# Two sets of the length-64 transform at a time, amid `down`, with a group's steps begun in the batch in front

## The chip, the cores and the metric

The kernel runs on one core of a Trainium2 chip. The metric is the device time of one launch in microseconds (us), the median of the runs made. TensorE (PE in the profile) multiplies matrices, VectorE (DVE) adds and multiplies element by element, ScalarE (ACT) copies and applies functions, GpSimd (POOL) does some additions and issues stores, and SyncE (SP) issues most of the loads and stores.

## The reference

Two blocks in a row, all in float32, with 8 batches, 3008 rows and 256 channels:

```
X = rfft(x, axis=1);  y = irfft(X * (filt_r + 1j * filt_i), n=3008, axis=1)      # filter along the rows
h = max(y^T @ w_tok1, 0) @ w_tok2;   u = y + h^T                                 # mixer along the rows, 3008 -> 256 -> 3008
out = u + max(u @ w_ch1, 0) @ w_ch2                                             # mixer along the channels, 256 -> 1536 -> 256
```

## The kernel before

**The filter** writes 3008 as 47 x 64. A first stage multiplies by the length-64 transform (the stage that the change is about), a second stage does the rest forward, the product with the filter and the way back, and the last step back is made inside the mixer. The first stage leaves its result in DRAM (`z_tmp`), the second loads it and leaves its own (`g_tmp`), which the mixer loads as tiles `t4`.

**The mixer** works batch by batch. `mix` loops over the batches, over six column tiles m of a batch (`MT`; five of 512 rows, the last of 448) and over six pairs jp of channel blocks (`JP`): 36 *items* a batch, 288 in all. Each item issues, in this order:

- place 0: `up_first` (four matmuls into two pg banks) and `up_middle` for this item, then `h_sums` and part 0 of `down` for the item in front; in some items also `u_part`, which makes the next m's `u` (`u_quarter` in batches 1 to 7);
- place 1: `up_last` (three matmuls into the same pg banks, two VectorE additions that take them out, two ScalarE activations), and up to two steps of a list of small VectorE steps (`finish`, `v_steps`);
- place 1.5: part 1 of `down` has been issued, part 2 not yet;
- place 2: part 2 of `down`, in jp 0 the first two steps of `finish` for the m in front, and in some items again `u_part`.

In batches 1 to 7 `u_part` comes at (jp, place) = (2, 2), (3, 0), (3, 2) and (3, 2); for the next batch's first m at (4, 0) and (5, 0), two parts each. In the item with number 32 of a batch (m 5, jp 2), `token_product` for the next batch runs: twelve steps of seven matmuls, whose weights `w1` lie in a ring of seven buffers. Seven loads are issued by SyncE in the items ahead, and the other five within `token_product`, each when a buffer comes free.

**Filter beside mixer.** The batches form groups, `GROUPS = ((0,), (1, 2), (3, 4), (5, 6), (7,))`. While a group is mixed, the filter's steps of the next group run in between. `dft(bs)` is a generator: it yields a letter for the kind of step that comes next, and the main loop looks at each place of `mix` whether that kind is due there. The order is written out by hand: no planner and no costs.

For the last three groups (12, 12 and 6 units `todo`, a unit is four columns of one batch) the first stage is *tiled*: a *set* is four matmuls of 64x64 tiles, each 512 wide, that run side by side in the four quarters of TensorE (eight instructions in the profile, line 523, helper `four`). The functions that take part:

- `x_pair` loads a unit of x into one of three `filt` buffers, with six DMAs or a few more on SyncE (L481 to L486); `more(n)` does so for the next n units;
- `x_sums` makes the sum and the difference of the two halves on VectorE (L548, two operations) in `p1` or `p2`, by the unit's parity;
- `a_pair` takes the two banks acc and b (`turn`), issues the set, and calls `z_out` for each bank: a ScalarE copy (L539) into a tile `t1` (two buffers) and a DMA on SyncE to `z_tmp` (L541).

The banks acc and b are also those of `u_quarter` (L865, L843) and of `token_product` (L810), through `free_bank`, which takes them in turn; the two pg banks are those of `up_first` (L944) and `up_last` (L960); the second stage's `bi_pair` uses them too.

In the kernel before, step "a" of the first stage is due at place 1 of every item from the first item of a group on: the x loads of three units in the first item, the sums of the first unit in the second, and then in each item the sums of the next unit, one x load, and a set with its copies. "w" (loads of the second stage) may come at any place, and "b" (a unit of the second stage) in the tiled groups at place 1.5 of jp 1 and 4, in the last six items of a batch (`tail`) of jp 1 and 3. The second stage already issues two sets in a row there: `b_pair` into acc and b, and `bi_pair` of the unit in front into pg.

Of the kernel before, what the change touches and what calls it, by code (L numbers as in the profile page):

```python
# [55 lines left out]
GROUPS = ((0,), (1, 2), (3, 4), (5, 6), (7,))  # L56
# [71 lines left out]
def kernel(  # L128
# [11 lines left out]
    nc = tc.nc  # L140
# [41 lines left out]
    def bank(tag):  # L182
        return (psg if tag == "pg" else psum).tile([P, 512], FP32, tag=tag, name="ps_" + tag)
# [3 lines left out]
    turn = ["acc", "b"]  # L187
# [233 lines left out]
    begin, copy, middle, end = (iter(tiles) for _ in range(4))  # L421
# [98 lines left out]
    def four(outs, stat, mov):  # L520
        for i in range(2):
            for j in range(2):
                nc.tensor.matmul(outs(i, j), stat(i, j), mov(i, j), start=True, stop=True)  # L523

    def half_of(half, n=HALF):
        return slice(half * HALF, half * HALF + n)

    def a_unit(b, c):
        ps = bank(free_bank())
        nc.tensor.matmul(ps, wa0 if b == 0 else wa, xs.pop((b, c)).rearrange("p a d -> p (a d)"), start=True, stop=True)  # L530
        if b == 0:
            d0, c = divmod(c, NXC // 2)
            nc.scalar.copy(out=turned[:, ts(c, 2 * XC), ds(d0 * P, P)], in_=ps.rearrange("p (a d) -> p a d", d=P))
            return
        z_out(b, ps, c, nc.scalar)

    def z_out(b, ps, c, q):
        t1 = t1p.tile([P, XC, D], FP32, tag="t1", name="t1")
        nc.scalar.copy(out=t1.rearrange("p a d -> p (a d)"), in_=ps)  # L539
        g, i = place_of[b]  # L540
        q.dma_start(z_d[g][:, ts(c, XC), i, :], t1)  # L541

    def x_sums(b, c, i):
        t = xs.pop((b, c)).rearrange("p s a d -> p s (a d)")
        where = (p1p, p2p)[i % 2]
        sd = where.tile([P, 2, XC * D], FP32, tag="p%d" % (1 + i % 2), name="sd")
        for e, op in enumerate((ALU.add, ALU.subtract)):
            nc.vector.tensor_tensor(out=sd[:, e], in0=t[:, 0], in1=t[:, 1], op=op)  # L548
        return sd

    def a_pair(b, c, sd):
        pss = [bank(tag) for tag in turn]
        four(lambda h, e: pss[h][half_of(e)], lambda h, e: was[half_of(h), e], lambda h, e: sd[half_of(h), e])
        for h in range(2):
            z_out(b, pss[h], 2 * c + h, nc.sync)

    def dft(bs):
        first = bs[0] == 0
        nb = len(bs)
        tiled = bs not in GROUPS[0:2]  # L560
        todo = [(b, c) for b in bs for c in range(NXC // 2 if tiled else NXC)]
# [18 lines left out]
        def w_load(c):  # L580
            table_load(c)
            (filt_load if first else filt_pair)(c)
# [3 lines left out]
        def more(n, queue=None):  # L586
            for i, u in to_load[0:n]:
                (x_pair if tiled else x_load)(*u, i, queue)
            del to_load[0:n]
# [2 lines left out]
        if bs == GROUPS[1]:  # L592
            ahead.append(more)
        if not first:
            yield "a"
        if tiled:
            sd = x_sums(*todo[0], 0)
            yield "a"
        for i, u in enumerate(todo):
            if tiled:  # L600
                now, sd = sd, x_sums(*todo[i + 1], i + 1) if i + 1 < len(todo) else None
                more(1)
                a_pair(*u, now)
                yield "a" if i + 1 < len(todo) else "w"
                continue
            if first and i in (0, 2):
                w_load(i // 2)
            if first and i in (6, 8):
                table_load(i // 2 - 1)
            a_unit(*u)  # L610
            if bs != GROUPS[1] or i >= XB:
                more(1)
            yield "a" if i + 1 < len(todo) else "w"
            if first and (i + 1) % (NXC // 2) == 0:

                for d in range(i // (NXC // 2) * P, (i + 1) // (NXC // 2) * P, 16):
                    v = turned.rearrange("p s d -> p d s")[:, d:d + 16, :]
                    nc.vector.transpose(v, v)
# [49 lines left out]
        def b_pair(c):  # L668
            pss, wb, t2 = two_banks(turn), wbs[c], t2s[c]
            four(lambda h, i: pss[h][half_of(i)], lambda h, i: wb[half_of(h, KH), i], lambda h, i: t2[half_of(h, KH), i])  # L670
            return pss
# [32 lines left out]
        if not first:  # L704
            last = K2 // KC
            for c in range(last):
                pss = b_pair(c)
# [457 lines left out]
    with tc.manual_schedule():  # L1165
        nc.sync.dma_start(wa0, wa0_d)
        nc.vector.memset(turned[:, A:K2, :], 0.0)
        for t in filts:
            nc.vector.memset(t, 0.0)
        half = 0  # L1170
        second = dft(GROUPS[1])
        for i, _ in enumerate(dft(GROUPS[0])):
            if i == 0:
                nc.scalar.dma_start(wai_t, wait_d)
            k = i - NXC - 2

            if i < NXC:
                if i in (1, 3, 5, 7, 9):
                    start()
                if i == NXC - 1:  # L1180
                    copies()
                    for t, src in ((wa, wa_d), (was, was_d), (wai, wai_d), (ident, ident_d)):
                        nc.scalar.dma_start(t, src)
            elif k >= 0:
                if k == K2 - 5:
                    pause.append(True)
                while half < 2 * IN_B * (k + 1) // K2:
                    if half % 2:
                        convert_end()
                    else:  # L1190
                        convert_middle()
                    half += 1

                if 19 <= k < 25:
                    t4_load(0, k - 19, 0, PARTS[1])
                elif 26 <= k < 29:
                    for c in range(2):
                        t4_load(0, 2 * (k - 26) + c, PARTS[1], PARTS[2])
                elif k in (30, 31):
                    for c in range(3):  # L1200
                        t4_load(0, 3 * (k - 30) + c, PARTS[2], PARTS[3])
        pause.clear()

        fill(5)
        for c in range(A // TC4):
            t4_load(0, c, PARTS[3], P, (nc.sync, nc.gpsimd)[c % 2])
        both = wcp.tile([P, 2, JP, 7, P], FP32, tag="wc", name="wc")

        chan.extend((both[:, 0], both[:, 1]))
        next(second)  # L1210
        for i in range(IN_B, A // 2 + TC * W2G):
            convert()
            if i == A // 2 + BY_PE - 1:
                sum_up()
                acc = token_sums(0)

        ahead[0](XF, nc.gpsimd)
        h1s[0] = token_relu(0, acc)
        for dh in range(DH):
            convert()  # L1220
            u_part(0, 0, dh)
        for f in v_steps(0, 0):
            f()
        convert_end(False)
        for _ in range(XB):
            next(second)
        group, todo, done = -1, iter(()), True

        def next_ready(b):
            return done or b != GROUPS[group][-1]  # L1230

        coming = "a"
        n = MT * JP
        for b, i, place in mix(next_ready):
            if group + 1 < len(GROUPS) and b == GROUPS[group + 1][0]:
                if not done:
                    raise AssertionError("the filter's steps don't fit beside the mixer's")
                group += 1  # L1240
                done = group + 1 == len(GROUPS)
                todo = iter(()) if done else dft(GROUPS[group + 1]) if group else second
                coming = "a"
            if done:
                continue
            jp = i % JP
            if coming in "aw":
                due = place == 1 or (place != 1.5 if group == 0 else coming == "w")
            elif group:
                tail = i >= n - JP  # L1250
                due = (jp, place) in {"b": ((1, 1.5), (3 if tail else 4, 1.5)), "m": ((2, 2) if tail else (3, 1), (5, 1)),
                                      "i": ((0, 1.5), (3 if tail else 4, 1.5))}[coming]
            else:
                due = (jp - (coming == "i")) % JP in ((5, 1, 2, 3) if i < 4 * JP else (5, 0, 1, 2, 3)) and place == {"b": 1, "m": 2, "i": 0}[coming]
            if coming == "a" and group == 0 and i < JP - 1:
                due = {0: 2, 1: 0, 1.5: 0, 2: 1}[place]
            for _ in range(due):
                if not done:
                    coming = next(todo, "end")
                    done = coming == "end"  # L1260
# [30 lines left out]
```

## Time and profile before

| | |
|---|---|
| median of 3 runs | 2424.17 us (2424.15 to 2425.02) |
| the profiled execution | 2425.85 us, span 2424.1 us |
| granted TensorE clock | 0.995 |
| TensorE busy | 2382.0 us (98%), 12340 matmul instructions |
| VectorE busy | 1942.6 us (80%) |
| ScalarE, GpSimd busy | 686.5 us (28%), 619.6 us (26%) |
| line 523, sets of the first stage | 30, from 493.18 us on (batches 1, 3 and 5) |

A page of a profile gives busy times by engine, a chain of work that ended last, and groups of instructions by source line. A row of the timeline gives the start, the length, engine, line, operation, output tile and inputs, the shape and how many of the kind were merged; in brackets stands how long the engine was idle before it and what ended that. Matmuls are pipelined: the length of one overlaps the next, so distances between starts are what counts.

### The profile page before, as it was taken

Reading aid. Unit: us, or ns where it says so; the run is one execution under the profiler, and the core shown is the slowest. Engines: PE = TensorE matmul, PEld = TensorE weight load, DVE = VectorE, ACT = ScalarE, POOL = GpSimd, SP = SyncE. Lnnn points to the kernel's source line nnn. Section 1 sums busy time; section 2 is a strip of 40 time slices with the busy share of each in tenths; the row PEclk is TensorE's granted clock in tenths of the full one; section 3 lists DMA queues with packets and bytes.
Section 4 is the critical chain, followed back from the end, with each engine's and each line's share of the span. In section 5 each row is a group of like instructions: output and inputs, shape, how many; then the busy total and the mean of one; then the engine's idle time right before and its main releaser. Section 6 shows DMA issues by size and latency. Waiting matters only on the chain.

```text
span 2424.1 us, 35550 instructions
## 1 busy us (share of the span) xinstructions
PE 2382.0 (98%) x12340; PEld 1985.9 (82%) x12340; DVE 1942.6 (80%) x3684; ACT 686.5 (28%) x1355; POOL 619.6 (26%) x1115
## 2 busy tenths in 40 slices
PE   7999999999999999999999999999999999999998
PEld 4666676978888888987888888897889888898887
DVE  7798778787887888777888888877787788777776
ACT  5733322232222222123222222213221222222222
POOL 7476332113111211211121112112112112112121
PEclk8999999999999999999999999999999999999999
DMA  9975545544343322444344222434324221411100
GB/s 217 248 231 166 155 144 177 161 155 138 108 133 98 86 79 78 160 134 146 103 132 125 76 81 82 145 101 133 90 75 151 63 60 46 152 63 31 39 15 20
DMA packets 187420, 278.66 MB, mean 115 GB/s; under 512 B 35485, under 2 KB 125291, under 8 KB 187240
## 3 DMA queue, kind: packets, MB, share of 16 engines
q1 hardware_dynamic: 140952, 212.56, 29.1%
q0 software_dynamic: 34688, 53.83, 8.2%
q10 hardware_dynamic: 11600, 10.00, 1.3%
q8 instruction: 98, 1.61, 0.3%
q14 instruction: 82, 0.67, 0.1%
HBM read 193.52 MB, written 82.72 MB: 114 GB/s over the span
## 4 chain that ended last, share of the span: by engine, by line
PE 90%; DVE 4%; DMA 2%; ACT 1%; issue 1%; POOL 1%; SPq 0%; ACTq 0%; DVEq 0%; POOLq 0%
PE ps_po L978 33%; PE ps_pg L944 18%; PE ps_pg L960 14%; PE ps_b L523 4%; PE ps_b L810 3%; PE ps_acc L865 3%; PE ps_acc L810 2%; PE ps_b L865 2%; PE ps_b L843 2%; PE ps_acc L843 2%; PE ps_pg L523 1%; PE ps_b L759 1%; DVE t L922 1%; DVE hh L922 1%; DMA filt<-in_x_dram 1%
## 5 line engine op out<-in xcount | busy, mean ns | idle before, releaser
L1025 POOL DMA_DIRECT2D out_dram<-r x752 | 407.9, 550 | 1542.3 <-issue 1082.2
L922 DVE TENSOR_TENSOR hh<-ps_pg,s 128x512 f32<-128x512 f32 (+3 forms) x864 | 482.0, 585 | 184.3 <-ACT s L947 181.4
L965 ACT ACTIVATE hh<-hh 128x512 f32<-128x512 f32 (+1 forms) x576 | 347.7, 621 | 993.4 <-DVE hh L922 989.5
L978 PE MATMUL ps_po<-t,wc 128*128 128x256 f32 (+1 forms) x2304 | 553.5, 379 | 1.8 <-DVE t L922 1.8
L978 PEld LDWEIGHTS ps_po<-t,wc 128*128 128x128 f32 x2304 | 427.8, 190 | 122.6 <-issue 40.8
L978 PE MATMUL ps_po<-hh,wc 128*128 128x256 f32 (+1 forms) x1728 | 413.2, 375 | 1.0 <-POOL wc L382 0.8
L944 PE MATMUL ps_pg<-v,wc 128*128 128x256 f32 (+1 forms) x1728 | 413.3, 375 | 0.7 <-POOL wc L381 0.7
L944 PEld LDWEIGHTS ps_pg<-v,wc 128*128 128x128 f32 x1728 | 327.3, 190 | 41.3 <-DVE v L922 3.1
L978 PEld LDWEIGHTS ps_po<-hh,wc 128*128 128x128 f32 x1728 | 327.7, 190 | 39.6 <-POOL wc L382 2.0
L960 PE MATMUL ps_pg<-u,wc 128*128 128x256 f32 (+1 forms) x1152 | 292.9, 377 | 1.2 <-DVE hh L922 1.2
L922 DVE TENSOR_TENSOR t<-t,hh 128x256 f32<-128x256 f32 (+1 forms) x576 | 245.0, 425 | 19.8
L960 PEld LDWEIGHTS ps_pg<-u,wc 128*128 128x128 f32 x1152 | 216.7, 190 | 44.2 <-DVE hh L922 13.9
L922 DVE TENSOR_TENSOR s<-ps_pg,hh 128x512 f32<-128x512 f32 (+1 forms) x288 | 196.1, 681 | 30.0
L947 ACT COPY s<-ps_pg 128x256 f32<-128x256 f32 (+1 forms) x288 | 105.9, 368 | 362.7 <-PE ps_pg L944 360.5
L922 DVE TENSOR_TENSOR t<-hh 128x512 f32<-128x512 f32 (+1 forms) x288 | 195.0, 677 | 0.6 <-ACT hh L965 0.6
L944 PE MATMUL ps_pg<-u,wc 128*128 128x256 f32 (+1 forms) x576 | 169.3, 375 | 2.9 <-DVE hh L922 2.8
L960 PE MATMUL ps_pg<-v,wc 128*128 128x256 f32 (+1 forms) x576 | 168.8, 375 | 0.0
L944 PEld LDWEIGHTS ps_pg<-u,wc 128*128 128x128 f32 x576 | 108.1, 190 | 19.3 <-DVE hh L922 6.2
L922 DVE TENSOR_TENSOR u<-ps_acc,u 128x256 f32<-128x256 f32 (+1 forms) x84 | 46.2, 550 | 97.0 <-PE ps_acc L865 66.1
L960 PEld LDWEIGHTS ps_pg<-v,wc 128*128 128x128 f32 x576 | 109.1, 190 | 12.7
L922 DVE TENSOR_TENSOR u<-ps_b,u 128x512 f32<-128x512 f32 (+2 forms) x126 | 74.4, 591 | 28.9 <-PE ps_b L865 26.7
L865 PE MATMUL ps_acc<-w 128*128 128x256 f32 (+1 forms) x336 | 85.5, 377 | 1.0 <-ACT t L539 1.0
(152 smaller groups left out, 2661.9 us busy)
## 6 DMA issues: line engine op xcount, KB each, us to landing
w<-w_tmp SPq DMA_DIRECT2D x84, 448.0 KB
w<-w_tmp SPq DMA_DIRECT2D x35, 896.0 KB
out_dram<-r POOLq DMA_DIRECT2D x696, 32.0 KB, 2.5
t<-g_tmp SPq DMA_DIRECT2D x42, 512.0 KB
g_tmp<-t SPq DMA_DIRECT2D x96, 192.0 KB
t<-z_tmp SPq DMA_DIRECT2D x180, 96.0 KB
z_tmp<-t SPq DMA_DIRECT2D x60, 256.0 KB
filt<-in_x_dram SPq DMA_DIRECT2D x90, 128.0 KB
```

The costliest lines, as they stand in the source:

```text
L523: nc.tensor.matmul(outs(i, j), stat(i, j), mov(i, j), start=True, stop=True)
L759: nc.tensor.matmul(acc[:, t, :], w1[:, a, ts(t, P)], t4[b, a // TC4][:, a % TC4, :], start=(a == 0 and t == 0), stop=(a == A - 1 and t == ...
L810: nc.tensor.matmul(ps[:, at], w[:, n], mov, start=(j == 0 and i in (0, 2)), stop=(j == AP - 1 and i >= 5))
L843: nc.tensor.matmul(ps[:, ds(q * P, n)], t4[b, c][:, r, ts(dh, P)], wai[:, 0:n], start=(first and q == 0), stop=(not first and q == 3))
L865: nc.tensor.matmul(ps[:, ds(j * hw, hw)], h1[:, n, :], w2m[m % 2][:, at, 0:hw], start=(i < 2 and j == 0), stop=(j == len(todo) - 1))
L922: nc.vector.tensor_tensor(out=out, in0=in0, in1=in1, op=op)
L944: nc.tensor.matmul(ps[:, 0:hw], chan[0][:, jp, n, :], mov, start=True, stop=True)
L947: nc.scalar.copy(out=s[:, 0], in_=g[0][:, 0, 0:hw])
L960: nc.tensor.matmul(ps[:, 0:hw], chan[0][:, jp, n, :], mov, start=True, stop=True)
L965: nc.scalar.activation(out=hs, in_=hs, func=AF.Relu)
L978: nc.tensor.matmul(po[i][:, j, 0:hw], chan[1][:, jp, n, :], mov, start=(jp == 0 and first == 1), stop=(jp == JP - 1 and last == 1))
L1025: q.dma_start(bass.AP(tensor=ob.tensor, offset=ob.offset + row * D + g * cw, ap=[[N1 * D, 32], [D if h else -D, n], [1, cw]]), blocks[ts(g ...
```

## The change

The first stage's units are taken two at a time, and its one kind of step is split into three:

- "s": the sums of one unit (VectorE);
- "d": both sets, one behind the other, the first into acc and b (`turn`), the second into the two pg banks; then the copies and stores of the pg banks (`leave_pg`), and the x loads of two more units;
- "c": the copies and stores of acc and b (`leave`).

Outside of the tail "s" is due at (jp, place) = (0, 1), (2, 1), (3, 1), (5, 1), "d" at (1, 1.5) and (4, 1.5), "c" at (2, 0) and (5, 0). In the tail "s" is due at (3, 1), (4, 0), (5, 1), "d" at (4, 1.5) and "c" at (4, 2). A group's generator now begins at item 32, place 1, of the last batch in front (just ahead of `token_product`): its first step, the x loads of three units, is issued there. The first pair of units then runs in the tail, and two pairs in each following m.

```diff
-    def a_pair(b, c, sd):
-        pss = [bank(tag) for tag in turn]
+    def a_pair(b, c, sd, tags):
+        pss = [bank(tag) for tag in tags]
         four(lambda h, e: pss[h][half_of(e)], lambda h, e: was[half_of(h), e], lambda h, e: sd[half_of(h), e])
-        for h in range(2):
-            z_out(b, pss[h], 2 * c + h, nc.sync)
+
+        def leave():
+            for h in range(2):
+                z_out(b, pss[h], 2 * c + h, nc.sync)
+
+        return leave
...
         if not first:
-            yield "a"
-        if tiled:
-            sd = x_sums(*todo[0], 0)
-            yield "a"
-        for i, u in enumerate(todo):
-            if tiled:
-                now, sd = sd, x_sums(*todo[i + 1], i + 1) if i + 1 < len(todo) else None
-                more(1)
-                a_pair(*u, now)
-                yield "a" if i + 1 < len(todo) else "w"
-                continue
+            yield "s" if tiled else "a"
+        for i in range(0, len(todo) if tiled else 0, 2):
+            sds = []
+            for j in (i, i + 1):
+                if j > i:
+                    yield "s"
+                sds.append(x_sums(*todo[j], j))
+            yield "d"
+            leave, leave_pg = [a_pair(*u, sd, tags) for u, sd, tags in zip(todo[i:i + 2], sds, (turn, ("pg", "pg")))]
+            leave_pg()
+            more(2)
+            yield "c"
+            leave()
+            yield "s" if i + 2 < len(todo) else "w"
+        for i, u in enumerate(() if tiled else todo):
...
         for b, i, place in mix(next_ready):
-            if group + 1 < len(GROUPS) and b == GROUPS[group + 1][0]:
+            at = (b, i, place)
+            if at == (0, 0, 0) or group + 1 < len(GROUPS) and at == (GROUPS[group][-1], n - 4, 1):
...
-                coming = "a"
+                coming = next(todo, "end") if group else "a"
+                if group:
+                    continue
...
                 tail = i >= n - JP
-                due = (jp, place) in {"b": ((1, 1.5), (3 if tail else 4, 1.5)), "m": ((2, 2) if tail else (3, 1), (5, 1)),
+                sums_at = ((3, 1), (4, 0), (5, 1)) if tail else ((0, 1), (2, 1), (3, 1), (5, 1))
+                due = (jp, place) in {"s": sums_at, "d": ((1, 1.5), (4, 1.5)), "c": ((2, 0), (4, 2) if tail else (5, 0)), "b": ((1, 1.5), (3 if tail else 4, 1.5)), "m": ((2, 2) if tail else (3, 1), (5, 1)),
                                       "i": ((0, 1.5), (3 if tail else 4, 1.5))}[coming]
```

## The prediction

> **What bounds the kernel now.** I read the page's engine shares and its chain first, then the timeline of TensorE (PE), VectorE (DVE) and SyncE's DMA queue where the change acts.
>
> ```profile
> PE 2382.0 (98%) x12340; PEld 1985.9 (82%) x12340; DVE 1942.6 (80%) x3684; ACT 686.5 (28%) x1355; POOL 619.6 (26%) x1115
> PE 90%; DVE 4%; DMA 2%; ACT 1%; issue 1%; POOL 1%; SPq 0%; ACTq 0%; DVEq 0%; POOLq 0%
> ```
>
> TensorE sets the end, so what the change is worth is what it adds to or takes from TensorE's own line of matmuls. VectorE is 80% busy and is the likeliest to hold it up. A set of length-64 matmuls (eight instructions of line 523) in the TensorE timeline:
>
> ```profile
> 492.66 0.59 PE L960 MATMUL ps_pg<-v,wc 128*128 128x256 f32 x2
> 493.18 0.65 PE L523 MATMUL ps_b<-sd,was 64*64 64x512 f32 x2
> ...
> 494.20 1.99 PE L978 MATMUL ps_po<-t,wc 128*128 128x256 f32 x8
> 496.52 1.13 PE L865 MATMUL ps_acc<-w 128*128 128x256 f32 x4 [0.33 <-ACT t L539]
> ```
>
> Full-size matmuls start every 0.216 us. The two of 492.66 would be followed at 493.09; the set starts at 493.18 (+0.09), lasts to 494.20 (1.02), and the eight of L978 behind it take 1.99 where eight undisturbed take 1.89 (+0.10). One set costs 1.22 us. Item starts (first matmul of `up_first`) confirm it: 7.260 us with a set, 6.043 without. The last line is a second cost: `u_quarter` waits for the bank that the set's second ACT copy still holds. The second stage already runs two sets in a row amid `down`:
>
> ```profile
> 627.05 1.03 PE L978 MATMUL ps_po<-t,wc 128*128 128x256 f32 x4
> 628.00 0.65 PE L523 MATMUL ps_b<-t,wb 48*64 48x512 f32 x2
> ...
> 629.88 1.13 PE L978 MATMUL ps_po<-t,wc 128*128 128x256 f32 x4
> ```
>
> Here 1.88 us lie between the first small matmul and the next full one, with the same margins; such items last 8.120 against 6.043, so two sets cost 2.08.
>
> **What the Trainium skill says.** "TensorEngine Tiling (Array Packing)", Key Properties: changing the tiling mode drains TensorE. The trace agrees: two sets apart cost 2.43, together 2.08. "TensorE: Matmul & The Clock Gate", Architectural detail: ScalarE and VectorE are strictly first in, first out. So a moved sum holds up every VectorE instruction behind it; at 528.78 in this trace the sums run between two other operations, and the next starts 1.21 us later. "DMA: Bandwidth & Descriptors", Anatomy of one DMA: a semaphore wait is made on the issuing sequencer. The trace agrees: at 479.12 and 481.34 SyncE's x loads wait for older loads to land, and nothing behind them is issued.
>
> **The change, part by part.** 30 sets (12, 12 and 6) become 15 pairs.
>
> *Tile switches.* 15 x (2.43 - 2.08) = **-5.3 us**, straight off TensorE's line.
>
> *Bank waits that go.* A set of before stands just ahead of `u_quarter`, which takes the same two banks. Item times minus the set: +0.60 us at channel pair 2 of the first m in each of three groups (1.8), +0.19 at pair 3 in five m (1.0). Now the banks are left at place 0 after each set pair, two items from the next `u_quarter`. **-2.8 us.** Together -8.1.
>
> *Sums at pair 0, place 1.* Sums (two of 0.68, pipelined: 1.21 us) used to lie in an item that a set made 1.22 longer. Now pairs 0, 2, 3, 5 carry sums with no set, 1 and 4 the sets. What pair 0 gives pair 1, VectorE in an undisturbed m:
>
> ```profile
> 2218.63 1.28 DVE L922 TENSOR_TENSOR hh<-ps_pg,s 128x512 f32<-128x512 f32 x2
> 2219.83 0.68 DVE L922 TENSOR_TENSOR u<-ps_po,u 128x512 f32<-128x512 f32 x1
> 2220.87 0.42 DVE L922 TENSOR_TENSOR r<-ps_po,r 128x256 f32<-128x256 f32 x1 [0.36 <-ACT r L990]
> ...
> 2222.47 0.41 DVE L922 TENSOR_TENSOR hh<-ps_pg,s 128x256 f32<-128x256 f32 x1
> 2222.98 0.69 DVE L922 TENSOR_TENSOR s<-ps_pg,hh 128x512 f32<-128x512 f32 x1
> 2223.59 0.68 DVE L922 TENSOR_TENSOR t<-hh 128x512 f32<-128x512 f32 x1
> ```
>
> The sums go in at 2219.83, in front of `finish`. `u` moves to 2221.04; the 0.36 of idle and its own slack absorb some, so `hh` starts 0.78 late, at 2223.25. `up_last` (its first matmul at 2223.52, weights asked for at 2223.30) waits for `hh`, ended at about 2223.7, and pays the 0.1 of a restart: +0.3. Its later matmul needs `s`, `down` needs `t`, both 0.78 late: +0.5 in all, and the set pair of pair 1 then covers the rest. Such sums come 7 times (3, 3, 1). In the first m of a batch the sums at (5,1) of the batch in front have already made VectorE 0.35 late: 0.87 three times, 0.5 four times. **+4.6 us** (2.5 to 6). Sums at pairs 2, 3 and 5 I cost at nothing: VectorE idles 0.84, 2.35 and about 2 us there before its next need.
>
> *The pair in the tail (last six items of batches 0, 2, 4).* The second sums come at (4,0), ahead of `up_last`'s additions, which free the two pg banks:
>
> ```profile
> 1038.18 1.15 DVE L922 TENSOR_TENSOR u<-ps_b,u 128x512 f32<-128x512 f32 x2
> 1039.24 1.14 DVE L922 TENSOR_TENSOR hh<-ps_pg,s 128x448 f32<-128x448 f32 x2
> ```
>
> The additions move to 1040.45 and end at 1041.6; the second set wants pg at 1040.8. +0.8. Then the ACT copies of the first set (4,2): tile t1 has two buffers, both in use by the pg copies until their z writes land (2.2 to 2.8 us after issue). The copies end 4.1 us behind the set, and ScalarE's `s` copy of pair 5 queues behind them; `u_quarter` part 2 wants the second bank at 3.5. +0.75 with its restart. In ordinary m these copies have until 7 us and wait hidden. 3 x 1.65 = **+4.9 us** (1.5 to 6).
>
> *SyncE's queue.* A group's first three x loads (18 DMAs) move from the next batch's start to the tail, in front of `token_product`, whose last five w1 loads are issued as it runs. In batch 0:
>
> ```profile
> 427.21 5.62 SPq L753 DMA_DIRECT2D t<-g_tmp  x6
> 432.87 12.81 SPq L787 DMA_DIRECT2D w<-w_tmp  x6
> ```
>
> SyncE is free at 434.15 (after the first of the six) and issues the w1 load of step 7 at 439.11. The 18 DMAs took 11.9 us in the trace (475.20 to 487.14). SyncE waits for the DMA eight back on its semaphores; here those are t4 and w1 loads that land at 439.5, 440.8 and 441.9. By that list the 18 end near 447.4; w1 then lands 3.4 to 3.9 us later, near 451, and step 7 starts at 448.29 in the trace, its weights asked for 0.2 earlier. **+2.9 us** (0 to 4). In batches 2 and 4 SyncE is free 12.6 and 13.7 us ahead of the first of these loads: the x loads end within 1 us of it, and w1 has 4 us to spare. Nothing.
>
> *At no cost:* later pairs' x loads (12 DMAs, about 6 us of SyncE, two items or more ahead of their sums); memsets on POOL and the second stage's first loads (they start an item later, 19 us ahead of the first use; in the last group about 3 us remain); z writes on SyncE (no wait until the next pair, 20 us on); out stores on POOL, untouched; the earlier end of the last group, as TensorE's work is the same.
>
> **Sum:** -8.1 + 4.6 + 4.9 + 2.9 = **+4.3 us**. The profiled execution has a span of 2424.1 and took 2425.85, 1.7 above the median of 2424.17; the difference goes on the median: 2428.4, +0.18%.
>
> **The rivals.** About 0.2%, 4.85 us, is what a measurement of this kernel can tell from no change.
>
> *The transfer is hidden anyway.* If the x loads end by 445 in batch 0, the w1 stall is gone: +1.4, 2425.5. For it: the ring is fast, 355 GB/s in that stage. Against: the landings named above.
>
> *The covers hold (faster).* The lag is absorbed, as at 490 in this trace, where a 0.6 lag cost `up_last` nothing, and bank waits in the tail are short: -8.1 to -4, around 2418. Against: pair 1 has less slack than the pair 2 of that place.
>
> *SyncE's queue blocks all three tails (slower).* If the 18 DMAs are held until after the w1 loads of batches 2 and 4 have lost their 4 us as well, two more stalls of 2.9: +10.1, 2434.3. It decides from about 5 us of waits more than the list gives. Against: the queue is idle from 1004 to 1011.
>
> *Not what it says:* sets at other places or steps that don't fit. By the table of places, tail pair, then two pairs an m, the second stage starts at the same item in two-batch groups; this I leave 0.02.
>
> **How the numbers follow.** The sum as worked out 0.45 (own range 2426.3 to 2430.5, half of it beyond 2429.0), transfer hidden 0.20, covers hold 0.16, three tails 0.17. Both signs are possible, so the range goes from 2419 to 2434: it leaves out most of "covers hold" and the far side of "three tails". Faster by over 0.2% 0.16; within 0.43 (transfer hidden and half of the sum); slower 0.41.
>
> **What would show it.** Items 1 and 4 of an m in the first stage at 8.12 us plus the lag, items 0, 2, 3, 5 at their undisturbed 6.04, 6.91, 9.99, 6.04; `up_last` waiting on `hh` in item 1; line 523 waiting on the additions in the tail, and L865 there on an ACT copy; L810 in batch 0 waiting on a w1 DMA. If item 1 shows 8.12 and the tail items no more than 2.1 us above before, the prediction is wrong on the fast side; if items 3 or 5 grow too, on the slow side.

## The result: slower by 0.56%

| | before | after |
|---|---|---|
| median | 2424.60 us (4 runs) | 2439.28 us (4 runs) |
| ratio, 95% interval | | 1.0056 (1.0045 to 1.0068) |
| profiled execution, time / span | 2425.85 / 2424.1 us | 2439.68 / 2437.9 us |

The forecast was 2428.4 with a range of 2419 to 2434: the sign was the one given 0.41, the size lay outside. All item times below are the distance between the first matmuls of `up_first` of two neighbouring items, in us.

The engine shares on the page of the kernel after:

```profile
PE 2387.9 (98%) x12340; PEld 1990.9 (82%) x12340; DVE 1943.9 (80%) x3684; ACT 691.5 (28%) x1355; POOL 623.3 (26%) x1115
```

TensorE has the same 12340 matmuls and is busy 5.9 us longer, although 15 sets no longer have tile switches of their own; the span is 13.8 us longer. So 7.9 us are new idle time, and some matmuls must have become slower, which busy time alone doesn't tell. Compared item by item, two places hold most of it.

**Batch 0, item 2 of the tail (its last six items, counted from 0): 24.19 became 32.34, +8.15.** First the TensorE timeline of the kernel after, then SyncE's (issue time, time to issue, what, count), then the windows (PE, PEld, DVE, ACT and POOL busy, granted clock, DMA share, GB/s):

```profile
447.78 0.39 PE L818 MATMUL ps_acc<-ts,w 128*128 128x128 f32 x2
453.58 1.22 PE L818 MATMUL ps_b<-t,w 128*128 128x128 f32 x4 [5.41 <-DMA w<-w_tmp]
...
456.73 1.06 PE L818 MATMUL ps_b<-t,w 128*128 128x128 f32 x4
...
458.84 0.39 PE L818 MATMUL ps_b<-ts,w 128*128 128x128 f32 x2
```

```profile
434.37 0.65 SPq L481 DMA_DIRECT2D filt<-in_x_dram  x1
...
448.37 0.26 SPq L484 DMA_DIRECT2D filt<-in_x_dram  x1
448.72 2.60 SPq L795 DMA_DIRECT2D w<-w_tmp  x5
```

```profile
448.00:451.90 3.90, 0.17 (x2) 0.00 (x0) 0.77 (x3) 0.00 (x0) 1.24 (x3) 1.00 0.84 244
452.00:455.30 3.30, 1.72 (x8) 1.72 (x9) 0.00 (x0) 0.00 (x0) 0.00 (x0) 0.50 1.03 403
455.40:458.80 3.40, 3.40 (x18) 3.40 (x17) 1.01 (x3) 0.00 (x0) 0.00 (x0) 0.50 0.37 148
458.90:462.00 3.10, 3.10 (x30) 3.10 (x30) 2.02 (x6) 0.00 (x0) 0.00 (x0) 1.00 0.00 0
```

The 18 x loads occupy SyncE from 434.37 to 448.63. The w1 load of step 7, at 439.11 before, is issued at 448.72 and lands at 453.54; TensorE waits 5.41 us. Then it runs at half speed: the clock column is 0.50 from 452 to 458.8, and four matmuls of L818 that take 0.61 at full clock (at 459.28) take 1.06 at 456.73. From 453.58 to 458.80 that is 5.2 us at half speed, so 2.6 us more. 5.4 + 2.6 = 8.0 of the 8.15.

**Batches 1 and 3, item 4 of the third m, the first set of the second stage: 7.26 became 9.16 and 9.45, +4.1 in all.** In batch 1, first GpSimd's and SyncE's timelines before, then after, then TensorE after in batch 3:

```profile
578.69 0.53 POOL L697 MEMSET filt<- 128x512 f32 x1 [6.74 <-DVE sd L548]
593.72 7.03 POOL L1025 DMA_DIRECT2D out_dram<-r  x13 [14.51 <-issue]
601.19 1.79 POOL L1025 DMA_DIRECT2D out_dram<-r  x3 [0.43 <-DMA out_dram<-r]
```

```profile
587.59 0.42 SPq L226 DMA_DIRECT2D filt<-in_filt_r_dram  x1
```

```profile
602.05 8.69 POOL L1033 DMA_DIRECT2D out_dram<-r  x16 [37.35 <-issue]
610.73 1.47 POOL L705 MEMSET filt<- 128x512 f32 x3
```

```profile
611.30 0.33 SPq L226 DMA_DIRECT2D filt<-in_filt_r_dram  x1
...
614.23 0.30 SPq L639 DMA_DIRECT2D t<-z_tmp  x1
```

```profile
1192.05 1.23 PE L523 MATMUL ps_b<-t,wb 48*64 48x512 f32 x4 [0.87 <-DMA t<-z_tmp]
1193.05 1.33 PE L523 MATMUL ps_acc<-t,wb 48*64 48x512 f32 x4
```

Before, each memset ran as soon as the sums had left its tile, ahead of the output stores. Now the three stand behind sixteen stores in GpSimd's queue. The filter loads write the same tiles and wait for them on SyncE; the z loads stand behind the filter loads, and TensorE waits for the z loads. The idle time in front of the set, 0.87 us, is only part of the 2.19: the two halves of the set, which start at 616.67 and 616.68 in a run without this wait (experiment 2, batch 1), start 1.00 us apart here, so the set itself takes about twice as long.

The rest is close to the prediction's terms and is set against them below.

### The profile page after: what moved, and what is told of

Its sections match the earlier page's. It is cut to its first block, busy times and chain, and to the rows that moved or that the text cites. A ratio compares the mean times of both kernels' runs of the same rounds, so it can differ in the third digit from the quotient of the medians.

```text
span 2437.9 us, 35547 instructions
## 1 busy us (share of the span) xinstructions
PE 2387.9 (98%) x12340; PEld 1990.9 (82%) x12340; DVE 1943.9 (80%) x3684; ACT 691.5 (28%) x1355; POOL 623.3 (26%) x1115
## 4 chain that ended last, share of the span: by engine, by line
PE 49%; DVE 1%; DMA 0%; SPq 0%; ACT 0%; issue 0%; DVEq 0%; POOL 0%; ACTq 0%
PE ps_po L986 20%; PE ps_pg L952 11%; PE ps_pg L968 8%; PE ps_b L818 2%; PE ps_acc L873 2%; PE ps_b L873 1%; PE ps_acc L818 1%; PE ps_b L523 1%; PE ps_pg L523 1%; PE ps_b L851 1%; PE ps_acc L851 1%; DMA z_tmp<-t 0%; DVE u L930 0%; DVE hh L930 0%; DVE sd L548 0%; DVE t L930 0%
## 5 line engine op out<-in xcount | busy, mean ns | idle before, releaser
L986 PE MATMUL ps_po<-t,wc 128*128 128x256 f32 (+1 forms) x2304 | 555.0, 379 | 1.8 <-DVE t L930 1.8
L986 PEld LDWEIGHTS ps_po<-t,wc 128*128 128x128 f32 x2304 | 428.3, 190 | 113.4 <-issue 46.9
L986 PE MATMUL ps_po<-hh,wc 128*128 128x256 f32 (+1 forms) x1728 | 413.5, 375 | 0.9 <-POOL wc L382 0.7
L986 PEld LDWEIGHTS ps_po<-hh,wc 128*128 128x128 f32 x1728 | 327.4, 190 | 40.6 <-POOL wc L382 1.9
```

Of the source, the lines that this page charges most:

```text
L986: nc.tensor.matmul(po[i][:, j, 0:hw], chan[1][:, jp, n, :], mov, start=(jp == 0 and first == 1), stop=(jp == JP - 1 and last == 1))
```

## The experiments

Theory: what the prediction missed is order in two queues, SyncE's in the tail of batch 0 and GpSimd's ahead of the second stage; the rest of its sum stands. Main rival: the moved loads compete for bandwidth or the second stage is simply begun too late, so that order alone gives nothing back. "Kernel after" is the changed kernel. Item times come from one profiled execution of each kernel, and experiments 1 to 4 have one timed execution each.

### 1. The group begins one place later

```diff
-... at == (GROUPS[group][-1], n - 4, 1):
+... at == (GROUPS[group][-1], n - 4, 2):
```

> Only the place at which a two-batch or one-batch group begins moves: from place 1 of the third-last item to place 2 of it, so that SyncE is given token_product's last w1 loads first and the group's 18 x loads behind them. Theory A (order in SyncE's queue): the w1 load of step 7 no longer waits behind the x loads, item 2 of the tail of batch 0 goes back from 32.34 us to 24.2 us and the time falls by about 8.1 us, to 2431; the granted clock stays at 1.00 there, because the wait that came ahead of its fall is gone. Rival B (the x loads and the w1 load share the bandwidth of the DMA engines): the w1 loads still land late in part, item 2 stays above 26 us. Rival C (the matmuls of the item themselves cost more): the item stays at 32 us.

Measured: item 2 at 24.195 (-8.15), and no fall of the clock in the tail. The time was 2436.77, only 2.5 us below the median of the kernel after, because batches 1 and 3 got worse: item 4 of the third m went to 9.76 and 11.51 (after: 9.16, 9.45), and item 5 behind the latter from 6.04 to 8.00. TensorE in batch 3, and the windows there:

```profile
1185.61 1.23 PE L523 MATMUL ps_b<-t,wb 48*64 48x512 f32 x4 [1.74 <-DMA t<-z_tmp]
1186.33 1.91 PE L523 MATMUL ps_acc<-t,wb 48*64 48x512 f32 x4
1188.17 2.07 PE L986 MATMUL ps_po<-t,wc 128*128 128x256 f32 x4
```

```profile
1186.00:1188.00 2.00, 2.00 (x8) 0.38 (x4) 1.07 (x1) 0.00 (x0) 0.00 (x0) 0.79 0.40 108
1188.00:1190.00 2.00, 2.00 (x5) 1.50 (x5) 1.38 (x2) 0.00 (x0) 0.00 (x0) 0.50 0.27 86
```

The wait for z was 0.9 us longer than in the kernel after, and the clock fell behind it: four L986 matmuls, 1.13 there, took 2.07 here. What follows: putting the x loads behind the w1 loads gives the whole of the 8.15 back, and the second place is unstable, not a fixed 1.9 to 2.2. Why z came later here than in the kernel after is open.

### 2. The memsets ahead of the output stores

```diff
+            if i + 2 >= len(todo):
+                zero()        # the three memsets, in the step of the last `leave()`
...
-        for c in range(FB):
-            if not first:
-                nc.gpsimd.memset(filts[c][:, :, 0, :], 0.0)
+        if not first and not tiled:
+            zero()
```

> Only the three memsets of the filter tiles on GpSimd move, to the step behind the last set pair of the tail, ahead of the sixteen out stores in GpSimd's queue. Theory A (GpSimd's queue: the memsets wait behind the stores, SyncE's filter loads wait for the memsets, the z loads wait behind the filter loads): the filter loads start about 12 us earlier, item 4 of the third m in batches 1 and 3 goes back from 9.16 and 9.45 us to 7.26 us, and the time falls by 4.1 us, to about 2435. Rival B (the second stage's step itself begins an item too late for its z loads): these items stay at 9.2 and 9.5 us, no change of time. Rival C (the z writes of the tail's set pair land late, and the z loads wait for them): no change either.

Measured: 2434.99; the two items at 7.260 each, the other items of that m unchanged from the kernel after. The filter loads, as SyncE's timeline of this kernel shows, start 12.6 us earlier:

```profile
598.70 0.37 SPq L226 DMA_DIRECT2D filt<-in_filt_r_dram  x1
```

GpSimd's queue is the cause. Both rivals (the step begins too late, z writes land late) fall: neither was touched. The stall in the tail stays: TensorE waits 4.78 us there, and item 2 lasts 31.99.

### 3. A group's first 18 x loads on GpSimd's queue

```diff
-        more(NXC if first else FB if tiled else XB)
+        more(NXC if first else FB if tiled else XB, nc.gpsimd if tiled else None)
```

> The group's first 18 x loads stay at their place in the program but are given to GpSimd's queue in place of SyncE's: same bytes, same time, another queue. Theory A (order in SyncE's queue): the w1 load of step 7 is issued near 439 again, item 2 of the tail of batch 0 falls from 32.34 us to about 24.2 us, the clock stays at 1.00, and the time is about 8 us below the changed kernel's (2431). Rival B (bandwidth): the x loads move in the same stretch as the w1 loads, so the stall stays in part: item 2 stays above 27 us and the w1 load takes more than 4.5 us from issue to landing.

Measured: item 2 at 24.195; the w1 load of step 7, issued at 440.47, took 3.84 us to land (3.92 before). GpSimd's queue in this run:

```profile
441.03 7.09 POOL L1033 DMA_DIRECT2D out_dram<-r  x13 [24.84 <-issue]
449.25 1.64 POOL L1033 DMA_DIRECT2D out_dram<-r  x3 [1.12 <-DMA out_dram<-r]
450.88 0.62 POOL L481 DMA_DIRECT2D filt<-in_x_dram  x1
```

The x loads stood behind sixteen output stores and were issued from 450.88 to 460.67, after that w1 load had landed. So they left SyncE's queue, but they did not move in the same stretch as in the kernel after, and this run doesn't set bandwidth against order as it was meant to. Other traces do. In the kernel after the w1 load was issued 9.9 us later in its item than before, and took 0.9 us longer to land. In experiment 1 the x loads followed right behind the w1 loads, from 445.67 on; the last three w1 loads took 6.35, 6.97 and 7.32 us to land (5.06, 4.84 and 4.75 before), and TensorE waited for none of them. So sharing makes a load land later, by up to 2.6 us here, but the stall comes from the late issue.

The time was not the expected one: 2440.02, since in batch 1 the wait for z grew to 3.01 us and the clock fell for 6.83 us, 5.6 us on top of the kernel after's. GpSimd's stores in front of the memsets paused there for 2.20 us, and SyncE's first filter load was issued 1.8 us into item 4, where the kernel after has it 0.4 us ahead of it; why the stores paused is open.

```profile
613.56 1.23 PE L523 MATMUL ps_b<-t,wb 48*64 48x512 f32 x4 [3.01 <-DMA t<-z_tmp]
614.50 1.66 PE L523 MATMUL ps_acc<-t,wb 48*64 48x512 f32 x4
616.09 2.07 PE L986 MATMUL ps_po<-t,wc 128*128 128x256 f32 x4
```

### 4. Two units' loads ahead of token_product

```diff
-        more(NXC if first else FB if tiled else XB)
+        more(NXC if first else FB - 1 if tiled else XB)
...
+                if j == 0:
+                    more(1)
```

> Of the group's first three x tiles only two (12 DMAs) are loaded ahead of token_product's last w1 loads; the third follows behind the first sums. SyncE should then reach the w1 load of step 7 some 3 us earlier (six DMAs at 0.5 us each). Theory A1 (the wait of 5.41 us costs 5.4 and the fall of the clock that follows it 2.6 us more): the wait is about 2.4 us, too short for the clock to fall, item 2 of the tail of batch 0 lasts about 26.6 us (2.4 above before), and the time is about 5.7 us below the changed kernel's, near 2433.5. Theory A2 (the clock's fall has nothing to do with the wait): the item lasts about 29.2 us, with the clock at 0.5 for some microseconds all the same.

Measured: 29.14, where A1 said 26.6 and A2 29.2, and a time of 2438.96, where A1 said 2433.5. Yet A2 is not what happened:

```profile
453.38 0.71 PE L820 MATMUL ps_b<-t,w 128*128 128x128 f32 x4 [3.05 <-DMA w<-w_tmp]
```

The wait was 3.05, not 2.4 (relative to the item's start SyncE reached the w1 load 1.8 us earlier than in the kernel after, not 3, and the load took 4.22 us to land, 0.6 less), and the clock fell all the same, at 454.5, a microsecond after work had begun again, for 3.41 us where it had fallen for 6.83. 3.05 + 3.41 / 2 = 4.75 of the 4.95 above the kernel before. A1 had the threshold wrong: a wait of 3.05 is enough. That the fall comes from the wait is borne out by experiments 1 and 3, where no wait and no fall are left in the tail.

### 5. Both moves (1 and 2) together

The three memsets stand just behind `leave()` here, in experiment 2 just ahead of it; its copies and stores are on ScalarE's and SyncE's queues, not on GpSimd's.

> The two moves together: the group begins one place later, behind token_product's w1 loads, and the memsets go ahead of the out stores. Theory A (the two queues are all that the prediction missed): item 2 of the tail of batch 0 at 24.2 us and item 4 of the third m in batches 1 and 3 at 7.26 us, so 8.15 + 4.1 us come off the changed kernel: 2424.3 + 14.6 - 12.2 = 2426.7, ratio to before 1.0008 to 1.0012, what the prediction's sum without its w1 stall gives (2425.5) and a little more. Rival B (the stalls that go expose others behind them): 2429 or more.

Measured, 20 runs beside 23 of the kernel before: ratio to before 1.0009 (1.0002 to 1.0016), medians 2427.64 and 2424.55. Items as expected: 24.19, 7.26, 7.26, and from 300 us to 2418 us no clock below 1.00 and no gap of TensorE over 0.8 us. So the two queues account for all that the sum had missed, as far as the runs can tell: the sum without its w1 stall, +1.4 us, is inside the interval (+0.5 to +3.9), though the medians differ by 3.1.

### 6. Odd units' sums on GpSimd (on top of 5)

These are the sums at pair 0, place 1, the tail's at pair 4, place 0, and also those at pair 3, place 1.

```diff
-            nc.vector.tensor_tensor(out=sd[:, e], ...)
+            (nc.gpsimd if i % 2 else nc.vector).tensor_tensor(out=sd[:, e], ...)
```

> The same two moves, and the sums of the odd units, those at pair 0 place 1 and at the tail's pair 4 place 0, on GpSimd in place of VectorE. Theory A (those sums hold up VectorE's queue: 0.89 us three times and 0.56 to 0.85 us four times in item 1, and 0.88 us three times in item 4 of the tail): items 1 go to 8.12 us and the tail's item 4 to 9.1 us, 5.2 + 2.6 = 7.8 us less than the kernel with the two moves alone, about 2419. Rival B (the small matmuls themselves, or their banks, make these items long): no change. Rival C (GpSimd takes much longer for the sums, so that the set pair waits): item 1 stays above 9 us.

Measured: one execution, 2423.57, where about 2419 was expected. Items 1 fell by 0.71, 0.56, 0.75, 0.71, 0.56, 0.56 and 0.71: 4.5 us, to 8.12 or 8.20 except in the first m, where 0.17 stay, probably the lag that the sums at (5,1) leave. So VectorE's queue is the cause there. In the tail nothing was won: item 4 stays, and item 5 grew by 0.40 and 0.43 in batches 0 and 2 and fell by 0.17 in batch 4. VectorE, then GpSimd, in batch 2:

```profile
1034.06 0.62 DVE L935 TENSOR_TENSOR s<-ps_pg,hh 128x448 f32<-128x448 f32 x1
1034.60 1.08 DVE L935 TENSOR_TENSOR t<-hh 128x448 f32<-128x448 f32 x1
1035.72 1.77 DVE L935 TENSOR_TENSOR t<-t,hh 128x224 f32<-128x224 f32 x2
1037.40 0.42 DVE L935 TENSOR_TENSOR u<-ps_acc,u 128x256 f32<-128x256 f32 x1
```

```profile
1033.93 2.88 POOL L548 TENSOR_TENSOR sd<-filt 128x512 f32<-128x512 f32 x2
```

GpSimd takes 2.88 us for the two sums, and two rows of VectorE's beside them take 1.08 and 1.77 where they take 0.61 and 0.82 in experiment 5. The set pair then waits 0.71 us for VectorE's `u`, and item 4 stays at 9.98. The Trainium skill, "GPSIMD Engine Reference", 1. Specifications, says that GpSimd shares its SBUF interfaces with VectorE, with contention where a VectorE instruction has two SBUF inputs or works in a two-port mode; these rows agree: the two slow ones read `t` and `hh`, both in SBUF, while the first, with one input in a TensorE bank, takes 0.62 as in experiment 5. For the tail's own 0.88 this run decides nothing, since it puts one delay for another.

### 7. Another tile for the late ACT copies (on top of 5)

```diff
-            ... zip(todo[i:i + 2], sds, (turn, ("pg", "pg")))]
+            ... zip(todo[i:i + 2], sds, ((turn, t3p, "t3"), (("pg", "pg"),)))]   # pool and tag handed on to z_out
```

> The same two moves, and the two late ACT copies of a set pair write to the two tiles t3, free in this stage, in place of t1, whose two buffers the pair's first copies hold until their z writes land. Theory A (ACT's copies wait for z writes in the tail, and `u_quarter` of pair 5 for the second bank): item 5 of the tail of batches 0, 2 and 4 falls by 0.4 to 0.75 us, 1.6 us in all; everything else stays. Rival B (item 5 is long for VectorE's lag): no change.

Measured: one execution, 2425.73; item 5 at 8.378 in all three tails, 0.45, 0.43 and 0.83 less, 1.7 us. ScalarE in the kernel after had shown the wait that goes:

```profile
1055.23 0.59 ACT L539 COPY t<-ps_b 128x512 f32<-128x512 f32 x1 [1.75 <-DMA z_tmp<-t]
```

### 8. The kernel before with the x loads alone moved

> The kernel before with one part of the change alone: the first 18 x loads of each two-batch or one-batch group go to SyncE three items from the end of the batch in front, in place of the next batch's first item; sets, sums and all else stay. Theory A (order in SyncE's queue, and the fall of the clock after it): item 2 of the tail of batch 0 goes from 24.19 us to 32.3 us, nothing in batches 2 and 4, second stage unchanged: 2424.3 + 8.1 = 2432.4. Rival B (the stall needs the earlier set pairs or sums as well): below 2427.

Measured: one execution, 2435.25, where 2432.4 was expected; item 2 of the tail of batch 0 at 33.24, +9.05, every item of batches 1 to 7 within 0.06 us of before. TensorE waits 6.33 us, and the clock falls for 6.83. The place costs as much without one set pair or moved sum; of the 0.9 us beyond the kernel after, 0.7 are SyncE's, which came to the w1 load at 450.07, that much later in its item, and 0.2 the load's own, which took 5.00 us to land. Why SyncE's waits were longer is open.

### 9. All mends together

Both moves, the other tile, and on GpSimd only the sums of units 3, 7 and 11 (`i % 4 == 3`), which are those at pair 0, place 1.

> The two moves, the other tile for the late ACT copies, and on GpSimd only the sums at pair 0, place 1 (units 3, 7 and 11); the tail's sums stay on VectorE. Theory A (the stalls are separate and add): item 1 as with all odd sums on GpSimd (4.5 us below the kernel with the two moves), the tail's item 5 at 8.38 us (1.7 us below), the tail's item 4 still 9.98 us, so 2427.6 - 6.2 = 2421.4, ratio to before 0.9985 to 0.9990: the change's own gain of 8 us less the tail's 2.6 and small rests. Rival B (VectorE is slowed while GpSimd works, as it was in the tail, so that later items give the gain back): 2424 or more.

Measured, 13 runs beside 17 of the kernel before: ratio to before 0.9991 (0.9983 to 1.0000), medians 2422.93 and 2425.18. Item 1 and the tail's item 5 did as expected: -4.4 and -1.7 against experiment 5. But item 0 of the first m rose by 0.88, 1.05 and 0.95. GpSimd, VectorE and TensorE where batch 2 ends and batch 3 begins:

```profile
1047.99 2.50 POOL L548 TENSOR_TENSOR sd<-filt 128x512 f32<-128x512 f32 x2 [14.53 <-DMA filt<-in_x_dram]
```

```profile
1049.31 1.73 DVE L935 TENSOR_TENSOR v<-u 128x512 f32<-128x512 f32 x1
```

```profile
1051.56 1.56 PE L957 MATMUL ps_pg<-v,wc 128*128 128x256 f32 x6 [1.03 <-DVE v L935]
```

GpSimd is idle and starts the sums of pair 0 as soon as the x load lands, an item early; VectorE's `v<-u` beside them takes 1.73 us, 0.68 in experiment 7, and TensorE waits 1.03 for it. Rival B holds for three items, 2.9 of the 6.1 us. The kernel is well ahead of the kernel after and about 2 us ahead of the one before, at the edge of what the runs can tell.

## Why the prediction was wrong

Right, term by term (predicted, then measured in items of the kernel after):

- *Tile switches and bank waits*, -8.1: items with a pair last 8.12 as in the second stage of before; items 2 and 3 lost 1.82 and 1.41 where a set of 1.22 left, so 0.60 three times and 0.19 five times. As written.
- *Sums at pair 0*, +4.6: 0.89 three times, 0.56 twice, 0.85 and 0.56 in the third m of batches 1 and 3: 5.2. Experiment 6 shows the cause.
- *The pair in the tail*, +4.9: item 4 pays 0.88 beyond the pair's 2.08, item 5 pays 0.41, 0.42 and 0.74: 4.2. (The two parts as written, 0.8 and 0.75, make 1.55 a tail and 4.65 in all, not 1.65 and 4.9.) Experiment 7 shows the cause of item 5; that of item 4, the sums ahead of `up_last`'s additions, stays argued.
- *Batches 2 and 4 pay nothing for SyncE*: item 2 there moved by less than 0.01. The rival "blocks all three tails" gave a slower time than the sum but by a stall that did not come.

These terms add up better than each fits: 0.6 too little for the sums and 0.7 too much for the tail cancel, which is luck.

Wrong, two steps:

- **SyncE's queue, "+2.9 us (0 to 4)", was 8.15.** The place, the batch and the mechanism were right (experiments 1, 3 and 8). Two errors add. First, the wait was sized 2.9 and was 5.41. The x loads ended at 448.63, not 447.4: the three loads for which SyncE waits landed at 440.06, 442.13 and 443.18, not at 439.5, 440.8 and 441.9, now that x loads moved beside them. And the w1 load took 4.81 us to land, not 3.4 to 3.9; in the trace of before only the first of the five took 3.92, and the other four, with no x load in front, took 4.65 to 5.06. Second, nothing stood in the sum for what a long wait does to the clock: 2.6 us. "TensorE: Matmul & The Clock Gate", What's actually happening, states that TensorE drops to half its clock after an idle window of about 3.4 us; the prediction cited this page for another sentence and did not ask it what a wait of 3 us or more costs. The upper bound of 4 was therefore no bound.
- **"At no cost: ... memsets on POOL and the second stage's first loads (they start an item later, 19 us ahead of the first use; ...)" cost 4.1.** The step was moved past sixteen stores in GpSimd's queue, and I counted its start, not its place in the queue. Out stores were named "untouched", in the same sentence, without asking what now stands behind them. SyncE's first filter load waited 12.3 us for the memsets, and the 19 us were gone (experiment 2).

With these at their true size, 4.3 + 5.25 + 4.1 = 13.7, against 13.8 in the profiled spans and 14.7 between the medians.

## What to carry to other kernels

When a step is moved, write down for each of its instructions the engine's queue and what stands in front of it there at the new place, memsets and waits included; a slack of 19 us at the start of a step says nothing if its first instruction is behind 8.7 us of stores. Price a long TensorE wait with the clock as well: each wait of 3.01 us or more in mid-kernel was followed by a fall here, and one of 1.74 too, and half of the time for which TensorE then works at 0.5 comes on top. And a helper engine that takes over work should be given it where the engine it helps is not reading the same memory: experiments 6 and 9 lost part or all of the gain where VectorE was.

## What the runs showed of the hardware

The fall of the clock is not proportional to the wait. Over all runs, away from the first and last stretches, it lasted 3.41 or 6.83 us, whole multiples of 3.41:

| wait of TensorE, us | clock at 0.5, us | where |
|---|---|---|
| 0.87, 1.28, 1.78 | none | second stage, batch 3: after, experiments 4 and 3 |
| 1.74 | 6.83 | second stage: experiment 1, batch 3 |
| 3.01 | 6.83 | second stage: experiment 3, batch 1 |
| 3.05 | 3.41 | tail of batch 0: experiment 4 |
| 4.78, 5.41, 6.33 | 6.83 | tail of batch 0: experiment 2, after, experiment 8 |

The page's figure of about 3.4 us agrees with the lengths; the waits that were enough are shorter than a whole idle window of that length, and 1.74 fell where 1.78 did not. The starts of the falls say more. In the kernel after they lie at 21.89, 110.64 and 451.97, and the last near the end at 2431.70: 26, 126 and 706 times 3.4133 us behind the first. In each of the eleven traces every fall begins such a whole number of stretches behind the first fall of the trace, to within 0.01 us. So the clock changes at fixed borders, 3.41 us apart, and not at a fixed time after a wait began.

That suggests that each stretch between two borders is judged by itself, with small matmuls counting little. The 1.74 us and the set behind them fill one stretch (1183.76 to 1187.17), while the 1.78 us have a border near their end (1191.99) and full-size matmuls for the first half of their stretch. As an estimate from the traces, each matmul was counted with its undisturbed time (0.216 us for 256 columns) and the part of the 128x128 array that it fills. Between 300 and 2400 us, the stretches just ahead of a fall were 0 to 29% filled by this count, and all other stretches at full clock 38% or more. The falls of 6.83 us are those in which TensorE was still waiting, or still at the small sets, in the first of the slow stretches; in the one of 3.41 us (experiment 4) it had full-size work all through. No run here was made to test this.
